# Sparse attention and a mixture of experts on one core: a token list cleared only behind each expert's tokens, weights loaded later, wider value rows

## The chip, the cores and the metric

The kernel runs on one core of a Trainium2 chip. The metric is the time of one execution on the device in microseconds, here the median of three runs. Matrix products run on TensorE (PE in the profile), reductions and elementwise work on VectorE (DVE), activations and casts on ScalarE (ACT), copies and indirect DMAs on GpSimd (POOL); SyncE (SP) issues nearly all direct DMAs. Data lie in the chip's memory (DRAM here), in SBUF (128 partitions) and in PSUM, where TensorE puts its results.

## The reference

```python
def _attn_ref(q, k, v, n_global, n_local):          # q, k, v: (4, 8, 768, 64); 8 globals, window 96
    scores = np.matmul(q, k.transpose(0, 1, 3, 2)) / np.sqrt(D)
    is_global = pos[None, :] < n_global
    is_local = (rel >= 0) & (rel < n_local)         # rel = query position - key position
    dist = np.where(is_global & ~is_local, float(n_local), np.abs(rel))
    scores = scores - slopes[:, None, None] * dist  # slopes = 2 ** -(h + 1), one per head
    scores = np.where(is_global | is_local, scores, -1e9)
    a = softmax(scores)                             # with 1e-9 added to the sum
    return np.matmul(a, v)

def _moe_ref(x, modality_id, w_gate, modality_bias, w1, w2):   # x: (3072, 512), 8 experts
    logits = x @ w_gate + modality_bias[modality_id]
    e_idx = np.argmax(logits, axis=1)
    gate_w = softmax(logits)[e_idx]                 # of the chosen expert
    for e in range(8):                              # w1: (8, 512, 1024), w2: (8, 1024, 512)
        h = np.maximum(x[e_idx == e] @ w1[e], 0.0)
        out[e_idx == e] = gate_w * (h @ w2[e])

def reference(...):                                 # heads of a token side by side: x
    return _moe_ref(_attn_ref(q, k, v, ...).transpose(0, 2, 1, 3).reshape(3072, 512), ...)
```

Everything is float32. Every query sees at most 96 earlier keys and 8 global ones; every token goes to one expert.

## The kernel before, in words

**Attention.** The 3,072 queries (4 batches of 768) are cut into 24 blocks of 128. `step(n)` writes the instructions of one block, with the scores of block n beside the value products of blocks n − 1 and n − 2. For each block SyncE loads queries (`qt`), keys (`kt`) and the value rows twice, once as they are (`va`) and once shifted by 32 positions (`vb`). A value row holds 8 heads of 64 numbers and a one each (`D1` = 65), so 520 floats or 2,080 bytes; `loadv` loads 128 such rows per tile, and `copyv` copies 64 of them on GpSimd into the tile of the block before. TensorE computes scores (L207), transposes probabilities (L274) and multiplies them with the values (L321). The result of a block, `xr`, is written to DRAM as 128 rows of `x_rows` (L352).

**Gate and token lists.** Behind each block come gate logits and the expert choice; behind each batch the positions of its tokens within their experts are worked out (`base` holds the running counts). Each token's number and gate are written by an indirect DMA on GpSimd (`route_c`, L455: 128 rows of 64 bytes from `tki`) into the DRAM list `ids_sorted`, in which every expert has its own stretch of rows. A unit of the second stage is 512 consecutive rows of this list. The last unit of an expert may read past the expert's tokens; it must find zeros there. For that the list is filled with zeros early: `consts_c` writes it from a tile of zeros, `zrow`, in eight DMAs of 196 KB on SyncE, placed at the steps 3 to 10 (`at(n, f)` puts f into step n, `last_work[n]` at the step's end).

**Experts.** A unit reads its list rows (`ld_x`, L594), gathers its rows of x on GpSimd (`gather_x`, L603), loads its expert's weights (`ld_w`: four raw tiles of 512 KB of the first layer, L623, and four of the second, L625), splits x and weights into a high and a low part of a shorter format, and does three products for each (L675 to L677, L714 to L716). Between the layers ScalarE applies the ReLU (L678, `hhe`) and VectorE forms its low part (L679, `hle`); at the end ScalarE scales by the gate (L731, `obe`; two buffers) and GpSimd scatters the rows to the output by an indirect DMA (L732). Two units, `e0` and `e1`, are formed from the first two batches and run first, while the last batch's tokens are still being routed; their tiles are `xge`, `rawe0a`, `rawe0b`, `rawe1a`, `rawe1b`. The next full unit is `s0` (`xgs`, `uis`).

**What sets the order.** TensorE, VectorE, ScalarE and GpSimd issue in the order in which the code is written in the parts around the change. SyncE's queue is put in order by a scheduler from the order in which the DMAs are written and from when their buffers come free. The raw weight tiles come from two pools in turn: `wraw` with 6 buffers, open during the attention, and `wrawb` with 2 buffers, which can be opened only when the attention's pool `a1` is closed. `ld_w` of the first unit's second layer, parts 0 and 1, stands at step `LAST` + 3 (`LAST` = 18), parts 2 and 3 at the end of step `LAST` + 5.

## Time and profile before

| | before |
|---|---|
| runs, us | 460.62, 463.5, 464.26; median 463.5 |
| profiled execution, us | 460.24, span of its instructions 458.4 |
| busy, share of the span | TensorE 92%, VectorE 55%, ScalarE 45%, GpSimd 28% |
| mean granted clock of TensorE | 0.983 |
| moved by DMA | 82.98 MB, of these 69.20 by SyncE's queue, 12.85 by GpSimd's |

All times of the trace below are those of the one profiled execution, counted from its first instruction. The attention's value products end about 165 us after it, and the experts' products fill the rest. A busy TensorE isn't TensorE at its peak, and a share of busy time over the span is a mean over stages with different limits. A wait "issue" is time in which an engine waited for nothing that the profile shows. The DMA share is the mean busy share of the core's 16 DMA engines. A time from issue to landing includes what a transfer waits behind others.

### The profile page before, as it was taken

The numbers are of one execution on the slowest core, as the hardware profiler recorded it, in microseconds if no ns is written. First come the engines' busy times: TensorE is split into PE (matmuls) and PEld (weight loads), VectorE is DVE, ScalarE is ACT, GpSimd is POOL, SyncE is SP. The second block draws the span as 40 slices with busy tenths as digits, with TensorE's granted clock in tenths as the row PEclk, the third lists the DMA queues.
The fourth block names the chain that finished last, engine by engine and source line by source line (L and its number), as shares of the span: only waits on it lengthen the run. The fifth ranks groups of instructions, "written<-read, shape, count | busy, mean of one in ns | idle before, by whom it ended". The sixth has DMA issues, their size and how long they took to land.

```text
span 458.4 us, 13462 instructions
## 1 busy us (share of the span) xinstructions
PE 420.8 (92%) x5391; PEld 337.9 (74%) x5391; DVE 252.4 (55%) x929; ACT 206.4 (45%) x459; POOL 129.5 (28%) x201
## 2 busy tenths in 40 slices
PE   7777989988868799999999999998999999999994
PEld 6565767766656567888888888886888886689983
DVE  5756978769949844887635073508535052331500
ACT  6546676655645332651534153418534152333410
POOL 8231225334355705454301132210100130021001
PEclk9899999999999789999999999999999999999999
DMA  8899987877774710641945162816724253821001
GB/s 275 274 351 338 299 242 242 271 228 229 241 287 143 246 55 4 232 162 52 371 139 200 69 231 75 268 63 220 270 92 162 92 186 118 297 95 46 1 24 51
DMA packets 41322, 82.98 MB, mean 181 GB/s; under 512 B 8571, under 2 KB 10003, under 8 KB 41252
## 3 DMA queue, kind: packets, MB, share of 16 engines
q1 hardware_dynamic: 36580, 69.20, 45.7%
q0 software_dynamic: 4672, 12.85, 7.9%
q8 instruction: 44, 0.72, 0.7%
q14 instruction: 26, 0.21, 0.1%
HBM read 67.64 MB, written 14.45 MB: 179 GB/s over the span
## 4 chain that ended last, share of the span: by engine, by line
PE 44%; issue 17%; POOL 3%; DMA 1%; DVE 0%; ACT 0%; POOLq 0%; DVEq 0%
PE phs L677 3%; PE phs L676 3%; PE phs L675 3%; PE phe L675 3%; PE poe L714 3%; PE pos L716 3%; PE poe L716 3%; PE pos L714 3%; PE poe L715 3%; PE pos L715 3%; PE phe L676 3%; PE phe L677 3%; POOL out L732 2%; DMA xge<-x_rows,uie 1%; PE mts L658 1%
## 5 line engine op out<-in xcount | busy, mean ns | idle before, releaser
L244 ACT ACTIVATE pr<-sc,nmx 128x128 f32<-128x128 f32 x192 | 61.0, 393 | 2.9 <-DVE nmx L228 2.9
L679 DVE SCALAR_TENSOR_TENSOR hls<-phs,hhs 128x512 fp32r<-128x512 f32 (+1 forms) x32 | 21.0, 658 | 71.2 <-ACT hhs L678 71.2
L675 PE MATMUL phs<-xhs,ahs 128*128 128x512 f32 (+1 forms) x128 | 48.4, 378 | 0.0
L677 PE MATMUL phs<-xhs,als 128*128 128x512 f32 (+1 forms) x128 | 48.1, 376 | 0.0
L714 PE MATMUL pos<-bhs,hhs 128*128 128x512 f32 x120 | 48.1, 400 | 0.0
L676 PE MATMUL phs<-xls,ahs 128*128 128x512 f32 (+1 forms) x128 | 48.1, 375 | 0.0
L716 PE MATMUL pos<-bhs,hls 128*128 128x512 f32 x120 | 46.9, 391 | 0.0
L715 PE MATMUL pos<-bls,hhs 128*128 128x512 f32 x120 | 46.8, 390 | 0.0
L228 DVE CUSTOM_DVE_ANT_0 sc<-s,tbl 128x136 f32<-128x136 f32 x192 | 44.2, 294 | 2.6 <-PE s L207 1.9
L732 POOL DMA_INDIRECT out<-obs,ois x15 | 14.9, 994 | 99.7 <-ACT obs L731 99.7
L207 PE MATMUL s<-kt,qt 64*32 64x136 f32 x1536 | 33.6, 283 | 7.9 <-issue 6.3
L678 ACT ACTIVATE hhs<-phs 128x512 fp32r<-128x512 f32 (+1 forms) x32 | 18.3, 572 | 48.7 <-PE phs L677 48.7
L455 POOL DMA_INDIRECT ids_sorted<-tki,pi x24 | 24.3, 1011 | 49.5 <-PE s L368 20.2
L321 PE MATMUL x<-vb,pT 128*32 128x65 f32 x768 | 31.0, 230 | 4.1 <-issue 2.2
L321 PE MATMUL x<-va,pT 128*32 128x65 f32 x768 | 30.8, 230 | 4.1 <-issue 4.0
L321 PEld LDWEIGHTS x<-vb,pT 128*32 128x32 f32 x768 | 27.5, 115 | 8.1 <-issue 5.4
L207 PEld LDWEIGHTS s<-kt,qt 64*32 64x32 f32 x1536 | 23.9, 106 | 12.3 <-issue 9.0
L281 ACT COPY pT<-pt 128x512 f32<-128x512 f32 x24 | 14.1, 586 | 40.5 <-PE pt L274 40.4
L274 PE MATMUL pt<-ident,pr 128*128 128x128 f32 x192 | 27.6, 285 | 4.4 <-ACT pr L244 2.8
L731 ACT ACTIVATE obs<-pos,uis 128x512 f32<-128x512 f32 x15 | 10.4, 692 | 43.5 <-PE pos L716 33.5
L321 PEld LDWEIGHTS x<-va,pT 128*32 128x32 f32 x768 | 27.2, 115 | 3.7 <-issue 3.5
L116 POOL COPY va<-va 64x520 f32<-64x520 f32 x24 | 14.7, 613 | 50.8 <-issue 42.5
(333 smaller groups left out, 972.4 us busy)
## 6 DMA issues: line engine op xcount, KB each, us to landing
va<-in_vr SPq DMA_DIRECT2D x25, 260.0 KB, 4.9
vb<-in_vs SPq DMA_DIRECT2D x25, 260.0 KB, 4.5
qt<-in_qs SPq DMA_DIRECT2D x24, 256.0 KB, 4.2
x_rows<-xr SPq DMA_DIRECT2D x24, 256.0 KB, 4.8
kt<-in_ks SPq DMA_DIRECT2D x20, 272.0 KB, 4.0
rawe0a<-in_moe_w SPq DMA_DIRECT2D x4, 512.0 KB, 5.6
rawe0b<-in_moe_w SPq DMA_DIRECT2D x4, 512.0 KB, 6.7
rawe1a<-in_moe_w SPq DMA_DIRECT2D x4, 512.0 KB, 5.3
```

The lines of the kernel that those rows point to most:

```text
L207: nc.tensor.matmul(ps[h][32 * j : 32 * j + 32, hp % 2 * W : hp % 2 * W + W], qt[hs, hp, 32 * j : 32 * j + 32], keys, start=True, stop=True,)
L228: V.tensor_tensor_reduce(out=sc, in0=pss[n, hp // 2][h][:, hp % 2 * W : (hp % 2 + 1) * W], in1=(tbl0 if n % NB == 0 else tbl)[:, hh, :], o ...
L244: last[0] = nc.scalar.activation(four(prs[n][:, hh, :], 32), four(scs[n][:, hx(hh), :])[:, :, 0:32], AF.Exp, bias=blk[n][:, hx(hh) : hx(hh ...
L274: nc.tensor.transpose(tp[:, j * P : (j + 1) * P], prs[n][:, hh, :], ident)
L321: nc.tensor.matmul(px[h][js, hp * D1 : (hp + 1) * D1], pT_of(n, hh)[:, js], vj[j][:, hh, :], start=False, stop=(hp == NP - 1), skip_group_ ...
L455: ins = nc.gpsimd.indirect_dma_start(out=ids, out_offset=bass.IndirectOffsetOnAxis(ap=pi[:, j : j + 1], axis=0), in_=tki[:, b * NB + j, :] ...
L675: nc.tensor.matmul(o, hi[:, fs], s.xh[:, c, 0:n], start=(c == 0), stop=False)
L676: nc.tensor.matmul(o, hi[:, fs], s.xl[:, c, 0:n], start=False, stop=False)
L677: nc.tensor.matmul(o, lo[:, fs], s.xh[:, c, 0:n], start=False, stop=(c == 3))
L714: nc.tensor.matmul(s.po[t], s.hh[:, fc, tt], hi[:, wv], start=(fc == 0), stop=False)
L715: nc.tensor.matmul(s.po[t], s.hh[:, fc, tt], lo[:, wv], start=False, stop=False)
L716: nc.tensor.matmul(s.po[t], s.hl[:, fc, tt], hi[:, wv], start=False, stop=(fc == 7))
```

## The change

Three edits.

1. *The list.* Each expert's stretch gets `ST` = 3,072 + 128 rows. The eight writes of zeros are gone; one write of 32 KB clears rows 0 to 511. A new function, `clear_ends`, is called once all counts are final: for each expert it computes the row behind its last token plus the partition number and writes 128 rows of zeros there, by one indirect DMA on GpSimd each, eight in all. Scatters of tokens and clears never touch the same rows, and are declared independent of each other.
2. *The first unit's second-layer weights.* Parts 0 and 1 are loaded at the end of the last step instead of step `LAST` + 3; parts 2 and 3 once `wrawb` is open.
3. *Value rows.* `vr` and `vs` are laid out with 528 floats (2,112 bytes) per row instead of 520, the last 8 unused; tiles `va` and `vb` have that width, and `copyv` copies 520.

```diff
-    ids = nc.dram_tensor("ids_sorted", (E * NT + U, IDW), I32, kind="Internal").ap()
+    ids = nc.dram_tensor("ids_sorted", (E * ST + U, IDW), I32, kind="Internal").ap()
...
-    va = [a1.tile([P, H, D1], F32, name=f"va{i}") for i in range(NV)]
+    va = [a1.tile([P, DV], F32, name=f"va{i}") for i in range(NV)]
...
-    nid = (E * NT + U) * IDW // P
-    zrow = a2.tile([P, nid // 8], I32, name="zrow")
-
-    def consts_c(j):
-
-        if not j:
-            nc.gpsimd.memset(zrow, 0)
-        idv = ids.rearrange("(p r) w -> p (r w)", p=P)
-        nc.sync.dma_start(idv[:, j * nid // 8 : (j + 1) * nid // 8], zrow)
+    zid = const.tile([P, U // P * IDW], I32, name="zid")
+
+    def consts_c():
+
+        nc.gpsimd.memset(zid, 0)
+        nc.sync.dma_start(ids[0:U].rearrange("(p r) w -> p (r w)", p=P), zid)
+
+    def clear_ends(pool, cnt):
+
+        end = pool.tile([P, E], F32, name="end")
+        V.tensor_tensor(end, cnt, ebase, ALU.add)
+        endi = pool.tile([P, E], I32, name="endi")
+        V.tensor_scalar(endi, end, pidx, None, ALU.add)
+        made = []
+        for e in range(E):
+            ins = nc.gpsimd.indirect_dma_start(
+                out=ids,
+                out_offset=bass.IndirectOffsetOnAxis(ap=endi[:, e : e + 1], axis=0),
+                in_=zid[:, 0:IDW],
+                in_offset=None,
+            )
+            for prev in made:
+                tc.declare_no_dep(ins.ins, prev.ins, reason="each expert has rows of its own")
+            made.append(ins)
+        return made
...
-    for j in range(8):
-        at(3 + j, consts_c, j)
+    at(3, consts_c)
...
-    at(LAST + 3, lambda: ld_w(eslots[0], "b", (0, 1)))
-    last_work[LAST + 5] = [(lambda: [gather_x(eslots[0], mark[0], (2, 3)), ld_w(eslots[0], "b", (2, 3))], ())]
+    last_work[NBLK] = [(lambda: ld_w(eslots[0], "b", (0, 1)), ())]
+    last_work[LAST + 5] = [(lambda: gather_x(eslots[0], mark[0], (2, 3)), ())]
...
     wrawb = sM.enter_context(tc.tile_pool(name="wrawb", bufs=RB, side="right", reuse_waits="tile"))
+    ld_w(eslots[0], "b", (2, 3))
...
+        for ins in clear_ends(plan, base[:, B - 1, NB, :]):
+            for prev in scat:
+                tc.declare_no_dep(ins.ins, prev.ins, reason="rows behind the last token of an expert")
+        yield
         r = yield from rest_plan(base[:, B - 1, NB, :], first_used)
...
-    laid["vr"] = rows.reshape(B, S, H * D1)
+    laid["vr"] = _np.zeros((B, S, DV), v.dtype)
+    laid["vr"][..., 0 : H * D1] = rows.reshape(B, S, H * D1)
```

The order of instructions on TensorE and ScalarE stays the same. Three places where it moves follow; a row is a source line, an operation and its operands, and line numbers of the change are two higher.

SyncE around the first unit's first-layer weights, before:

```order
L623 DMA rawe0a_3166<-in_moe_w 128x1024
L623 ISA
L623 DMA rawe0a_3168<-in_moe_w 128x1024
L352 DMA x_rows<-xr_3057 128x512
L99 DMA qt_3227<-in_qs 128x512
L625 ISA
L625 DMA rawe0b_3472<-in_moe_w 128x2x512
L625 ISA
L625 DMA rawe0b_3474<-in_moe_w 128x2x512
L592 TENSOR_LOAD uoie
```

and with the change:

```order
L625 DMA rawe0a_3159<-in_moe_w 128x1024
L625 ISA
L625 DMA rawe0a_3161<-in_moe_w 128x1024
L354 DMA x_rows<-xr_3050 128x512
L101 DMA qt_3220<-in_qs 128x512
L594 TENSOR_LOAD uoie
```

The two second-layer loads have left the place behind the last query block; the loads of the first-layer weights ahead of them stay.

SyncE from the reading of the unit's list rows (`uie`) on, before:

```order
L594 DMA uie_3543<-ids_sorted 128x4x2
L594 ISA
L594 DMA uie_3554<-ids_sorted 128x4x2
L625 ISA
L625 DMA rawe0b_3884<-in_moe_w 128x2x512
L352 DMA x_rows<-xr_3728 128x512
L625 ISA
L625 DMA rawe0b_3886<-in_moe_w 128x2x512
L352 DMA x_rows<-xr_3878 128x512
L623 ISA
L623 DMA rawe1a_4224<-in_moe_w 128x1024
```

and with the change:

```order
L596 DMA uie_3543<-ids_sorted 128x4x2
L627 ISA
L627 DMA rawe0b_3959<-in_moe_w 128x2x512
L627 ISA
L627 DMA rawe0b_3961<-in_moe_w 128x2x512
L354 DMA x_rows<-xr_3717 128x512
L354 DMA x_rows<-xr_3867 128x512
L354 DMA x_rows<-xr_3955 128x512
L627 ISA
L627 DMA rawe0b_4046<-in_moe_w 128x2x512
L627 ISA
L627 DMA rawe0b_4048<-in_moe_w 128x2x512
```

Parts 0 and 1 stand where part 2 stood, parts 2 and 3 behind the last three writes of `x_rows`; the second unit's first-layer loads (`rawe1a`) come only behind them.

GpSimd behind the gathers of the second unit, before:

```order
L455 DMA ids_sorted<-tki,pi_4153 25088x16 x6
L603 DMA xge_4240<-x_rows,uie_3554 128x512 x4
L732 DMA out<-obe_4469,oie_4172 3072x512
L455 DMA ids_sorted<-tki,pi_4343 25088x16 x6
L732 DMA out<-obe_4607,oie_4172 3072x512
L732 DMA out<-obe_4637,oie_4172 3072x512
```

and with the change:

```order
L457 DMA ids_sorted<-tki,pi_4146 26112x16 x6
L605 DMA xge_4233<-x_rows,uie_3543 128x512 x4
L1078 DMA ids_sorted<-zid,endi 26112x16 x8
L734 DMA out<-obe_4465,oie_4165 3072x512
L457 DMA ids_sorted<-tki,pi_4336 26112x16 x6
L734 DMA out<-obe_4612,oie_4165 3072x512
L734 DMA out<-obe_4642,oie_4165 3072x512
```

The eight clears (L1078) stand ahead of the first output and of the last batch's six scatters.

## Rows read from the trace of the kernel before

**Rows 1.** Windows: stretch, length, busy us per engine, granted clock, DMA share, GB/s

```profile
27.00:46.00 19.00, 15.27 (x485) 11.53 (x468) 12.16 (x75) 10.79 (x36) 4.45 (x9) 1.00 1.02 345
46.00:92.00 46.00, 42.34 (x1393) 33.32 (x1392) 37.84 (x228) 31.03 (x98) 16.71 (x35) 1.00 0.84 263
...
117.00:145.00 28.00, 20.33 (x629) 15.67 (x632) 20.69 (x113) 15.60 (x49) 12.62 (x15) 1.00 0.75 253
145.00:168.00 23.00, 18.77 (x385) 14.62 (x367) 15.97 (x52) 8.24 (x21) 11.64 (x19) 0.78 0.48 157
168.00:458.00 290.00, 282.14 (x1340) 230.30 (x1338) 128.16 (x245) 110.31 (x158) 59.44 (x58) 1.00 0.41 140
```

**Rows 2.** Waits of PE, 27 to 46 us: total, times, longest

```profile
PE x L321 <- issue: 1.6, 2, 1.1
PE pt L274 <- issue: 1.1, 1, 1.1
PE s L207 <- issue: 0.7, 1, 0.7
```

**Rows 3.** Timeline of SP's DMA issues: start, us, line, transfer, count

```profile
27.97 2.66 SPq L1068 DMA_DIRECT2D ids_sorted<-zrow  x4
...
121.55 1.29 SPq L625 DMA_DIRECT2D rawe0b<-in_moe_w  x2
...
150.37 0.37 SPq L625 DMA_DIRECT2D rawe0b<-in_moe_w  x1
...
153.91 1.89 SPq L623 DMA_DIRECT2D rawe1a<-in_moe_w  x2
```

**Rows 4.** DMA queues: kind, packets, MB, share of 16 engines

```profile
q8 instruction: 44, 0.72, 0.7%
```

**Rows 5.** Timeline of PE: start, us, work, [idle before <- releaser]

```profile
127.61 0.22 PE L321 MATMUL x<-va,pT 128*32 128x65 f32 x1 [2.01 <-issue]
...
133.94 0.55 PE L274 MATMUL pt<-ident,pr 128*128 128x128 f32 x3 [2.80 <-ACT pr L244]
```

**Rows 6.** Timeline of ACT ahead of the second of these

```profile
131.67 1.28 ACT L244 ACTIVATE pr<-sc,nmx 128x128 f32<-128x128 f32 x4
```

**Rows 7.** Waits of PE, 145 to 168 us

```profile
PE mte L658 <- DMA xge<-x_rows,uie: 1.6, 2, 1.1
```

**Rows 8.** DMA issues by transfer: count, KB each, median us from issue to landing

```profile
va<-in_vr SPq DMA_DIRECT2D x25, 260.0 KB, 4.9
vb<-in_vs SPq DMA_DIRECT2D x25, 260.0 KB, 4.5
...
kt<-in_ks SPq DMA_DIRECT2D x20, 272.0 KB, 4.0
...
ids_sorted<-tki,pi POOLq DMA_INDIRECT x24, 2.3
...
out<-obe,oie POOLq DMA_INDIRECT x8, 2.8
```

**Rows 9.** Timeline of POOL: first output, last of six scatters

```profile
198.91 1.03 POOL L732 DMA_INDIRECT out<-obe,oie  x1 [9.68 <-ACT obe L731]
...
207.14 0.97 POOL L455 DMA_INDIRECT ids_sorted<-tki,pi  x1 [0.30 <-issue]
```

**Rows 10.** Timeline of ACT: first cast, fourth output scaling, first ReLU of e1

```profile
183.27 1.05 ACT L645 CAST bhe<-rawe0b 128x1024 fp32r<-128x1024 f32 x1
...
214.83 0.69 ACT L731 ACTIVATE obe<-poe,uie 128x512 f32<-128x512 f32 x1 [4.75 <-PE poe L716]
217.50 0.60 ACT L678 ACTIVATE hhe<-phe 128x512 fp32r<-128x512 f32 x1 [1.98 <-PE phe L677]
```

**Rows 11.** Timeline of DVE: behind the final counts, and e1's first low part

```profile
195.82 1.23 DVE L646 TENSOR_TENSOR ale<-rawe1a,ahe 128x1024 fp32r<-128x1024 f32 x1
...
218.13 0.69 DVE L679 SCALAR_TENSOR_TENSOR hle<-phe,hhe 128x512 fp32r<-128x512 f32 x1 [2.60 <-ACT hhe L678]
```

**Rows 12.** Timeline of PE: fifth block of e1's first layer, first transpose of s0

```profile
225.46 0.39 PE L675 MATMUL phe<-xhe,ahe 128*128 128x512 f32 x1
...
239.07 0.60 PE L658 MATMUL mts<-ident,xgs 128*128 128x128 f32 x4
```

## The prediction

> **What bounds the kernel now.** I read the windows first [rows 1]. From 168 us to the end TensorE is busy 282.14 of 290 us with the two layers of the experts at a granted clock of 1.00: work to be done, and the change leaves that engine's order as it is. What can be won lies ahead of it, in the attention stages, where TensorE is busy 15.27 of 19, 42.34 of 46, 20.33 of 28 and 18.77 of 23 us. Whatever makes the attention end earlier moves the whole rest forward, since the expert stage has next to no idle time that could swallow it.

> Next, the waits of TensorE by stretch. From 27 to 46 us its idle time is put down to "issue", 1.6 + 1.1 + 0.7 = 3.4 us [rows 2]: no engine and no transfer that the profile links to an instruction released it. In this stretch the DMA engines are at a share of 1.02, 345 GB/s, and the issues of SyncE show why: eight writes of zeros of 196 KB, the first four at 27.97 [rows 3], go out among the loads of the blocks.

> What is such an "issue" wait? The queues hold a candidate: 44 packets, 0.72 MB, so 16 KB each, of kind instruction [rows 4]. The engines' programs come through the same DMA engines as the data. If TensorE's next piece of program stands behind data, TensorE stands still and nothing in the dependences shows it. This is a reading, not a fact. For it: such waits lie where the DMA share is high. The stretch from 168 on has a share of 0.41 and an idle time of 7.86 us in 290.

> The stretch from 117 to 145 has the two longest ones: TensorE resumes at 127.61 after 2.01 us of "issue", and at 133.94 after 2.80 us [rows 5]. The second is put down to ScalarE's exponentials, but the four of them began at 131.67 and took 1.28 us together [rows 6], so they were over at 132.95, 1.0 us before TensorE went on. Here too something else came last. Ahead of both, at 121.55, SyncE issues two loads of the first unit's second-layer weights (`rawe0b`), 512 KB each [rows 3], behind 2 MB of its first-layer weights. Last, from 145 to 168, TensorE waits 1.6 us for the gather of the unit's rows (`xge`) [rows 7], while the fourth such load (150.37) and two first-layer loads of the second unit (153.91) are on their way [rows 3].

> **The sum, part by part**, against the profiled run's 460.24 us (span 458.4), which is 3.3 below the median of 463.5; I take the difference over to the median.

> *Zeros.* 1.57 MB leave the stretch from 27 to 46. At its 345 GB/s that is 4.6 us of transfers. TensorE's 15.27 us of work, at the next stretch's busy share (42.34/46 = 0.92, DMA share 0.84), would take 16.6 instead of 19 us [rows 1]: −2.4. At most all the issue waits go, −3.4; at least one of 0.7 [rows 2]. I take −2.4, the next stretch being the nearest picture of the same work without zeros. The 32 KB that remain cost nothing that shows.

> *Second-layer weights 0 and 1.* Two loads, 1 MB, leave the place at 121.55 and come behind the reads of the lists, where one such load stood before. The 2.01 us wait I leave standing: the 2 MB of first-layer weights are still ahead of it. The 2.80 us wait stands behind the removed megabyte (3.0 us at 345 GB/s); I take −2.7, with 0 and −4.8 (both waits) as ends. In the new place a megabyte could make a wait of its own, up to 2.0 as at 127.61. I take 0: the DMA share from 145 to 168 is 0.48, the lowest of the attention stretches [rows 1]. What hides their later landing: ScalarE casts the first of them at 183.27 [rows 10], 40 us later.

> *Weights 2 and 3.* They move behind the attention's last value product, and on SyncE's queue the four first-layer loads of the second unit now stand behind them. Both pairs have cover: they are read from 183.27 on [rows 10], and the second unit's first-layer weights only once the first unit is computed. If that cover went, the price would be a landing, some 5 us. The gathers `xge` lose 1.5 MB of competitors: their wait of 1.6 can go whole (−1.6) or stay (0). I take −1.6. [...]

> *Value rows.* 50 loads grow by 1.5%, 0.2 MB in all, 0.6 us of transfers at 345 GB/s, spread over 24 blocks. No row shows this width. The nearest ones: `va` lands in 4.9 us and `vb` in 4.5, `kt` with rows of 2,176 bytes and 272 KB in 4.0 [rows 8]. So longer rows aren't dearer as such, and between +0.6 and a gain (rival B) I take +0.3. [...]

> *The clears.* Two VectorE steps more, and eight indirect DMAs on GpSimd between the second unit's gathers and the first output. There GpSimd is idle (9.68 us ahead of the output at 198.91), and a scatter of the same kind takes 0.97 us of it, 1.27 with the gap behind it [rows 9]: 8 × 1.27 = 10.2 us. The counts are final with the vector step before 195.82 [rows 11]; with that step's 1.23 and the two new ones the clears start at 197.6 and end at 207.8. What is queued behind them: output 0 (to 209.1), six scatters (7.6, to 216.7), output 1, which lands 2.8 us later [rows 8], at 219.5. It frees the buffer for ScalarE's fourth output scaling, at 214.83 before (0.7); behind that on ScalarE stands the ReLU of 217.50 (0.6) [rows 10], then VectorE's step of 218.13 (0.69) [rows 11]. That chain now ends at 221.5. TensorE wants the PSUM bank for 225.46 [rows 12]: 3.9 us to spare, cost 0. The list read and the gathers behind these outputs slip by up to 5 us; their first reader stands at 239.07 [rows 12], 24 us behind the scaling. Bounds: 0, and rival C.

> Sum: −2.4 −2.7 −1.6 −0.5 +0.3 = −6.9, so 453.3 for a run like the profiled one and **456.5** against the median. The ends that I hold likely together give 452 to 460.

> **Rivals.**
> A: the issue waits aren't made by this traffic. Against it speaks that the stretch with the zeros has the highest share; for it, that the stretch from 117 to 145, at 0.75, idles more than that from 46 to 92, at 0.84: 7.67 of 28 us against 3.66 of 46 [rows 1]. Also, a wait that goes may only return at the next piece of program. What is left is the gather's 1.6: **462**. [...]

> B: the wider rows also land faster. If `va` and `vb` came down to the 4.0 of `kt` [rows 8], each block's loads would be through 0.9 and 0.5 us sooner, and the 2.01 us wait that I left standing [rows 5] and half of the 3.66 us of idle time from 46 to 92 [rows 1] might go as well. I estimate another 4 us: **452.5**. For it speaks only that the narrower row is the slower one; against it, that `kt` is also fetched at other moments.

> C, the slower side: the clears hold GpSimd longer than the scatters did. With c for each clear and scatter the chain above ends at 203.7 + 14c; from c = 1.55 on it passes 225.46. Were each to hold the engine for the 2.3 us of its landing [rows 8], it would end at 235.9 and TensorE stand for 10.5 us. With the fetch terms at their low ends (0.7 and 0) and the gather's 1.6: **471**. Against it speaks that six scatters in a row were issued at 1.27 [rows 9]; for it, that fourteen in a row don't occur before.

> **Numbers.** Forecast 0.55, A 0.25, B 0.13, C 0.07. The range from 450 to 463.5 leaves out C, the lowest part of B and the upper edge of A. Some 1% of the time (4.6 us) is what a measurement of this kernel can tell from no change. The forecast passes it in five sixths of its cases (0.46), B always, A hardly (0.03): faster 0.62. C gives slower nearly always: 0.07. The rest, 0.31, is within 1%.

> **What would show it.** Right: TensorE's issue waits between 27 and 46 us fall to about 1; the wait before the transposes at 133.94 is gone while the 2.01 us one stays; no `xge` wait; the fourth output scaling held for some 5 us until the second output has landed, and no idle time of TensorE before its step at 225.46. Wrong: waits of the same length at other places in the attention (A); `va` and `vb` landing near 4.0 (B); TensorE released by ScalarE or VectorE in the second unit's first layer (C). What would make it wrong most simply is that a fetch, put off no longer by zeros, meets the next block's loads instead.

## The result, and the profile after

The changed kernel took 457.81 us (median of 15 runs, 454.85 to 460.69), the kernel before 464.77 us (15 runs, 460.62 to 467.14): ratio 0.9858, 95% interval 0.9827 to 0.9888, so 6.6 us less by the ratio. The forecast was −6.9. On another chip the very same program was 1.7% slower than the kernel before; that is the last experiment, and the more important half of what follows.

The profiled execution of the change has a span of 454.7 us, 3.7 less than that of before. One execution of each says less than the medians: the profiled run of before (460.24) lies 4.5 below its median.

Windows of the change (columns as in [rows 1]); the last two rows are a second cut, around the second unit's first layer:

```profile
27.00:46.00 19.00, 15.94 (x495) 12.29 (x495) 12.32 (x75) 11.11 (x36) 4.32 (x8) 0.92 0.85 282
46.00:92.00 46.00, 41.95 (x1343) 32.44 (x1343) 36.50 (x222) 29.96 (x96) 15.96 (x33) 1.00 0.81 246
...
117.00:145.00 28.00, 24.61 (x806) 19.71 (x805) 22.83 (x124) 17.64 (x57) 14.80 (x20) 0.97 0.71 231
145.00:168.00 23.00, 19.34 (x370) 14.14 (x356) 16.55 (x53) 9.53 (x24) 11.33 (x18) 0.93 0.67 223
168.00:454.00 286.00, 278.60 (x1317) 227.67 (x1315) 126.29 (x243) 108.61 (x155) 69.98 (x66) 1.00 0.42 140
...
166.00:215.00 49.00, 49.00 (x242) 39.81 (x241) 35.69 (x138) 17.58 (x27) 26.73 (x26) 1.00 0.29 104
215.00:237.00 22.00, 22.00 (x101) 18.23 (x100) 11.56 (x17) 10.71 (x16) 9.25 (x8) 1.00 0.79 283
```

The gain stands where the weights were: from 117 to 145 us TensorE gets 806 matmuls done instead of 629, and from 145 to 168 the granted clock is 0.93 instead of 0.78. Since the two kernels have drifted apart by then, a window no longer holds the same work in both; counted from the start, the change is 135 matmuls behind at 117 us and 24 ahead at 168. From 27 to 46, where the zeros were, the DMA share fell from 1.02 to 0.85 and the traffic from 345 to 282 GB/s, yet TensorE's busy time rose only from 15.27 to 15.94 us, and from 46 to 92 it did 50 matmuls fewer than before.

TensorE's waits in the change, of the stretches 27 to 46 (three rows), 117 to 145, 145 to 168 and 168 to the end:

```profile
PE pt L276 <- issue: 1.6, 1, 1.6
PE x L323 <- issue: 0.8, 1, 0.8
PE s L209 <- issue: 0.7, 1, 0.7
...
PE x L323 <- issue: 1.6, 1, 1.6
...
PE x L323 <- POOL vb L119: 1.9, 1, 1.9
PE mte L660 <- DVE xle L664: 1.0, 1, 1.0
...
PE pog L718 <- DVE hlg L708: 1.7, 2, 0.9
```

Against [rows 2]: 3.1 us of issue waits from 27 to 46 where there were 3.4. Against [rows 5]: the wait of 2.80 us is gone, the one of 2.01 is there with 1.6. Against [rows 7]: no wait for `xge`, but 1.0 us for VectorE's split of the same rows. The 1.9 us put down to GpSimd's copy of value rows (`vb`) isn't new; the trace of before has it from 145 to 168 us too:

```profile
PE x L321 <- POOL vb L117: 1.9, 1, 1.9
```

So the megabyte that now stands behind the list reads made no wait of its own. Behind 168 us TensorE waits for nothing that the clears could have made.

How transfers land, and the data queue (columns as in [rows 8]):

```profile
q1 hardware_dynamic: 35572, 67.83, 46.0%
...
va<-in_vr SPq DMA_DIRECT2D x25, 264.0 KB, 3.0
vb<-in_vs SPq DMA_DIRECT2D x25, 264.0 KB, 2.8
```

The medians of `va` and `vb` look like a large gain from the wide rows (4.9 and 4.5 in [rows 8]). They are medians of those few loads that something waited for, three of each here, seven and eight before. The queue shows no gain: 46.0% of 16 engines' 454.7 us for 67.83 MB, 49.3 us of an engine per MB; before it was 45.7% of 458.4 us for 69.20 MB, 48.4.

The clears in the timeline of the change: first clear, second output, fourth output scaling and first ReLU of the second unit, the fifth block of its first layer, and SyncE's first loads for the next unit:

```profile
194.17 0.99 POOL L1078 DMA_INDIRECT ids_sorted<-zid,endi  x1 [8.49 <-DVE lib L504]
...
214.09 1.00 POOL L734 DMA_INDIRECT out<-obe,oie  x1 [0.30 <-issue]
...
217.07 0.69 ACT L733 ACTIVATE obe<-poe,uie 128x512 f32<-128x512 f32 x1 [8.45 <-DMA out<-obe,oie]
217.66 0.59 ACT L680 ACTIVATE hhe<-phe 128x512 fp32r<-128x512 f32 x1
...
221.90 0.39 PE L677 MATMUL phe<-xhe,ahe 128*128 128x512 f32 x1
...
215.90 2.58 SPq L625 DMA_DIRECT2D raws0a<-in_moe_w  x4
```

The chain over GpSimd went as forecast: the fourth scaling waits 8.45 us for the second output, the ReLU follows at once, and TensorE goes on without a gap 4.2 us later.

### The profile page after: what moved, and what is told of

Read it like the earlier page. It is cut to its first block, busy times and chain, and to the rows that moved or that the text cites. A ratio compares the mean times of both kernels' runs of the same rounds, so it can differ in the third digit from the quotient of the medians.

```text
span 454.7 us, 13466 instructions
## 1 busy us (share of the span) xinstructions
PE 420.7 (93%) x5391; PEld 336.9 (74%) x5391; DVE 251.3 (55%) x931; ACT 206.3 (45%) x459; POOL 139.8 (31%) x209
## 3 DMA queue, kind: packets, MB, share of 16 engines
q1 hardware_dynamic: 35572, 67.83, 46.0%
## 4 chain that ended last, share of the span: by engine, by line
issue 33%; PE 25%; POOL 6%; DVE 1%; DMA 1%; POOLq 0%; ACT 0%; SPq 0%
POOL out L734 3%; PE phe L677 3%; PE poe L716 3%; PE poe L718 3%; PE phe L679 3%; PE poe L717 3%; PE phe L678 3%; POOL xgs L605 2%; PE phs L678 1%; PE phs L677 1%; PE phs L679 1%; DMA uis<-ids_sorted 1%; PE x L323 1%; PE mte L660 1%; PE mts L660 0%
## 5 line engine op out<-in xcount | busy, mean ns | idle before, releaser
L677 PE MATMUL phs<-xhs,ahs 128*128 128x512 f32 (+1 forms) x128 | 48.4, 378 | 0.0
L209 PE MATMUL s<-kt,qt 64*32 64x136 f32 x1536 | 34.9, 290 | 7.4 <-issue 5.8
L733 ACT ACTIVATE obs<-pos,uis 128x512 f32<-128x512 f32 x15 | 10.4, 692 | 43.5 <-PE pos L718 33.2
```

Source lines behind the costliest of these rows:

```text
L209: nc.tensor.matmul(ps[h][32 * j : 32 * j + 32, hp % 2 * W : hp % 2 * W + W], qt[hs, hp, 32 * j : 32 * j + 32], keys, start=True, stop=True,)
L677: nc.tensor.matmul(o, hi[:, fs], s.xh[:, c, 0:n], start=(c == 0), stop=False)
```

## The experiments

Four groups of runs, each on one chip, with the kernel before on the same chip. The last column is read from each profile's timeline: the time from the first product of the first unit's second layer (`poe`) to the first transpose of the next unit (`mts`); before, 190.80 to 239.07 = 48.27.

| run | what | ratio to before, 95% | `poe` to `mts`, us |
|---|---|---|---|
| the change | | 0.9858 (0.9827 to 0.9888) | 48.26 |
| e1, chip 2 | clears alone | 1.0164 (1.0125 to 1.0203) | 56.36 |
| e2, chip 2 | weights alone | 0.9915 (0.9883 to 0.9947) | 48.25 |
| e3, chip 2 | rows alone | 1.0010 (0.9975 to 1.0044) | 48.25 |
| e4, chip 2 | all but the clears | 0.9926 (0.9896 to 0.9955) | 48.27 |
| e5, chip 15 | all but the weights | 1.0015 (0.9980 to 1.0049) | 48.28 |
| e6, chip 15 | clears alone, late | 0.9992 (0.9955 to 1.0030) | 48.28 |
| e7, chip 15 | the change, clears late | 0.9881 (0.9829 to 0.9932) | 48.26 |
| e8, chip 15 | the change, GpSimd delayed | 0.9876 (0.9825 to 0.9926) | 48.26 |
| e9, chip 5 | clears alone again | 1.0173 (1.0125 to 1.0221) | 56.91 |
| e10, chip 5 | the change and 1 MB of copies | 1.0158 (1.0122 to 1.0194) | 56.89 |
| e11, chip 5 | the change, first-layer loads spaced | 1.0082 (1.0045 to 1.0120) | 57.31 |
| e12, chip 0 | the change again | 1.0172 (1.0127 to 1.0217) | 57.90 |

**One edit at a time (e1 to e4).** Each is the kernel before with the hunks of one edit, e4 with those of two:

```diff
 e2:
-    at(LAST + 3, lambda: ld_w(eslots[0], "b", (0, 1)))
+    last_work[NBLK] = [(lambda: ld_w(eslots[0], "b", (0, 1)), ())]
...
+    ld_w(eslots[0], "b", (2, 3))
 e3:
+DV = H * D1 + 8
 e1 (and left out in e4):
-        at(3 + j, consts_c, j)
+        for ins in clear_ends(plan, base[:, B - 1, NB, :]):
```

> The kernel before with the first edit alone: eight writes of zeros (1.57 MB) out of 27 to 36 us, eight clears on GpSimd at 198 us. Theory 1 (the forecast: TensorE's program stood behind the zeros): -2.4 us, ratio 0.995, and fewer issue waits of TensorE from 27 to 46 us. Theory 2 (the waits come back at the next pieces of program, as in the one profile of the change, where block 7 of the attention begins at 46.96 instead of 46.16 us): 0 +- 1 us, ratio 1.000, the sum of issue waits over the attention as before. Theory 3 (the edit carries the whole gain): -6.5 us, ratio 0.986.

> The kernel before with the second edit alone: second-layer weights of the first unit loaded at the end of the last step and behind the attention. Theory 1 (the forecast: -2.7 for the program that stood behind them, -1.6 for the gather, -0.5 for the clock): -4.8 us, ratio 0.990; the wait of 2.8 us before the transposes of block 20 is gone. Theory 2 (only the gather and the clock behind the attention): -2 to -3 us, ratio 0.995. Theory 3 (rows or zeros carry the gain): 0, ratio 1.000.

> The kernel before with the third edit alone: value rows of 2,112 bytes. Theory 1 (the forecast): +0.3 us, ratio 1.000 to 1.001, the queue of SyncE takes 1.5% longer for these rows. Theory 2 (rival B: wider rows land faster and the program fetches behind them too): -3 to -4 us, ratio 0.992.

> The change without its first edit: the eight writes of zeros are back, the weights are late and the value rows wide. If the edits add up and theory 1 of each holds: ratio to before 0.990 (-4.5 us). If the zeros cost nothing that lasts: 0.986, as the whole change. If the zeros carry the gain: 1.000.

Rows: no change in time, theory 1. Weights: −0.85%, 4.0 us, near theory 1's 4.8. Clears alone: none of the three theories; 1.6% slower. The table's last column says where: 8.1 us between `poe` and `mts`, a stretch whose length is otherwise the same to 0.03 us. e4 came out as the first of its three ratios (0.990, if the edits add up). It is e2 with wide rows, and both have the zeros: that they agree says once more that the rows do nothing, and nothing of the zeros.

**Does the order on GpSimd make that loss? (e5 to e8)** e5 leaves the weights at their old places, so it is e1 with wide rows. e6 and e7 hold the clears behind the second output, e8 lengthens the chain:

```diff
 e6, e7:
+        while len(scaled) < 2:
+            yield
         for ins in clear_ends(plan, base[:, B - 1, NB, :]):
+            behind(ins, scaled[1])
 e8, in clear_ends:
+        nc.gpsimd.tensor_copy(idle, bm(end, 256))
```

> The change without its second edit: clears and wide rows, the first unit's second-layer weights at their old places. The clears alone had cost 1.6%, and the change with everything but the clears had gained 0.7%, the whole change 1.4%. Theory 1 (the clears only pay when the weights are late: with the old places the second unit's first layer stands still between 230 and 240 us): ratio to before 1.014 to 1.018, and a stretch from the first unit's second layer to the next unit's transposes of some 56 us instead of 48. Theory 2 (the loss of the clears alone was an accident of that program's placement in time, and the edits add up): ratio 0.992 to 1.000.

> The kernel before with the first edit alone, the eight clears on GpSimd held behind the second output scaling, so that they stand behind the six scatters and the second output instead of ahead of them; wide rows and late weights left out. Theory 1 (the clears ahead of the second output hold ScalarE's fourth scaling and with it TensorE in the second unit's first layer): the 8 us that the clears alone lost come back, ratio 0.995 to 1.000, no idle time of TensorE between 225 and 245 us. Theory 2 (the loss has nothing to do with GpSimd's order): ratio 1.016 as with the clears ahead.

> The whole change, the eight clears behind the second output. Theory 1 (in the whole change the chain over GpSimd has slack left, and the clears cost nothing where they are): same as the change, ratio to before 0.983 to 0.989; the gathers of the next unit come some 5 us later and still ahead of their reader. Theory 2 (the clears cost something in the change as well): below 0.983.

> The whole change with one copy of 128 x 2048 numbers more on GpSimd ahead of the clears, some 2.4 us, so that clears, scatters and the second output come about as late as in the kernel with the clears alone. Theory 1 (a chain with 3.9 us of slack as forecast): no loss, ratio to before 0.983 to 0.990. Theory 2 (the point from which it decides lies lower, between the change and the clears alone, and behind it the loss is 8 us at once): ratio 1.000 to 1.006, TensorE standing in the second unit's first layer.

e5: theory 2, no loss; edits that lost 1.6% on chip 2 lose nothing on chip 15. e6 can therefore not tell its theories apart: there was nothing to bring back. e7 and e8 are as the change: with the clears moved out of the chain or with the copy ahead of it (1.90 us in the profile, by which the first clear comes 1.7 us later behind the first `poe`) nothing changes. Of the 3.9 us of slack that the forecast gave the chain, at least these 1.7 are there.

These four also measure the weights a second time, on one chip and without the long stretch: e8 against e5 (0.9876 to 1.0015) and e7 against e6 (0.9881 to 0.9992) differ by the place of the weights, and otherwise only by edits that cost nothing here. That is 1.4 and 1.1%, some 6 and 5 us, more than e2's 4.0, though with ratios known to some 0.5% the two measurements don't exclude each other.

**Repeat, and two tests of traffic (e9 to e11).** e9 is e1, word for word. e10 adds traffic at the old place of the weights, e11 spreads the 2 MB that are left there:

```diff
 e10:
+            nc.sync.dma_start(
+                spd[c],
+                w2[ds(eslots[0].e, 1), 2 * c * P : 2 * (c + 1) * P, :].rearrange("o (a p) d -> p (o a) d", p=P),
+            )
 e11:
-    last_work[LAST] = [(lambda: ld_w(eslots[0], "a", (0, 1)), ())]
+    last_work[LAST + 1] = [(lambda: ld_w(eslots[0], "a", (1,), last[0]), ())]
```

> The kernel with the clears alone once more, word for word the same. It had lost 1.6%, of this 8.1 us in one place of the experts' stage where TensorE, ScalarE and SyncE went forward in steps of 0.7 us for 8 us; the same edit with wide rows beside it lost nothing. Theory 1 (the loss belongs to this program, whatever run it is): ratio 1.013 to 1.020, the same place, 56 us from the first unit's second layer to the next unit's first transpose. Theory 2 (it belonged to that loading of the program): ratio 0.995 to 1.003, and 48.3 us there.

> The whole change, with two copies of 512 KB each from DRAM to DRAM more on SyncE's queue, at the place from which the second-layer weights were taken; nothing reads what they write, so that nothing but the traffic is added. Theory 1 (1 MB of traffic at this place makes TensorE wait, through its program's fetch and the loads behind it): 2 to 4 us of the gain are lost, ratio to before 0.992 to 0.996, and an issue wait of 2.5 us or more is back between 120 and 140 us. Theory 2 (the gain came from the gathers and the clock behind the attention alone): as the change, 0.986 to 0.988.

> The whole change, the first unit's four first-layer loads (2 MB, issued within 4 us before) one to a block of the attention. Theory 1 (traffic in a lump makes the waits): the wait of some 1.6 to 2.0 us that the change left in block 20 goes, -1.5 to -2 us against the change, ratio to before 0.982 to 0.985. Theory 2 (the wait comes back at the next pieces of program, as with the zeros): as the change, 0.986 to 0.988. Theory 3 (the last load comes too late for GpSimd's cast, and the gathers behind it): slower than the change.

e9 lost the same 1.7% in the same place. e10 and e11 carry the clears, and both have the long stretch too, which neither expectation had foreseen, so their totals against before say little about traffic. What can be read is TensorE's waits between 117 and 145 us. The first fence is of e10, the second of e11 (its last two rows, behind the dots, are of 145 to 170 us), the third, for comparison, of the change on chip 0 (e12):

```profile
PE x L324 <- issue: 4.1, 6, 2.3
```

```profile
PE x L323 <- issue: 2.4, 6, 0.5
...
PE x L306 <- DVE xr L347: 2.3, 1, 2.3
PE x L323 <- issue: 1.1, 1, 1.1
```

```profile
PE x L323 <- issue: 3.5, 4, 2.4
```

With the megabyte put back the longest wait is 2.3 us, without it 2.4: no wait of 2.5 us or more came back, against theory 1. Both stand where the trace of before waits 2.01 us, behind the first-layer loads; what the megabyte did at the place of the 2.80 us is told below, under "What an issue wait is". Spread, the longest wait there falls to 0.5, as theory 1 has it, but the two rows behind it, of 145 to 170 us, show what is late next: 2.3 us for VectorE's `xr` and an issue wait of 1.1. On the same chip e11 took 470.06 us and e10 473.36.

**The chip or the program? (e12)** By then the profiles fell in two kinds. In one, nearly every scatter on GpSimd during the attention is followed by a short stop of TensorE; in the other none is.

> The change itself once more, unaltered. In seven kernels of two of the three earlier groups of runs (chips 2 and 5) TensorE stands still for some 0.5 us at the end of nearly every indirect DMA of GpSimd in the attention, and the four of them that have the clears lose 8 to 9 us in the second unit's first layer; in the other group (chip 15) and in the change's own profile neither shows. Theory 1 (it belongs to the chip on which a program runs, not to the program): if the short stops show on this chip, the change has 56 to 57 us there instead of 48.3 and is at 1.004 to 1.012 of the kernel before; if they don't, it is at 0.984 to 0.990 with 48.3 us. Theory 2 (it belongs to the programs): no short stops and no long one, 0.984 to 0.990 on any chip.

The change itself, unaltered, at 1.0172: theory 1. Its timeline; first two pairs of a scatter and the stop behind it, then the second unit's first layer:

```profile
77.84 0.98 POOL L457 DMA_INDIRECT ids_sorted<-tki,pi  x1 [1.52 <-PE s L370]
79.15 0.22 PE L323 MATMUL x<-va,pT 128*32 128x65 f32 x1 [0.43 <-issue]
83.74 0.98 POOL L457 DMA_INDIRECT ids_sorted<-tki,pi  x1 [2.71 <-PE s L370]
85.06 0.24 PE L323 MATMUL x<-vb,pT 128*32 128x65 f32 x1 [0.46 <-issue]
...
199.40 1.00 POOL L1078 DMA_INDIRECT ids_sorted<-zid,endi  x1 [10.60 <-DVE lib L504]
...
219.90 1.00 POOL L734 DMA_INDIRECT out<-obe,oie  x1 [0.30 <-issue]
...
222.79 0.69 ACT L733 ACTIVATE obe<-poe,uie 128x512 f32<-128x512 f32 x1 [7.85 <-DMA out<-obe,oie]
231.38 0.60 ACT L680 ACTIVATE hhe<-phe 128x512 fp32r<-128x512 f32 x1 [7.89 <-remote]
...
222.78 0.48 PE L677 MATMUL phe<-xhe,ahe 128*128 128x512 f32 x1 [0.59 <-issue]
224.22 0.47 PE L678 MATMUL phe<-xle,ahe 128*128 128x512 f32 x1 [0.95 <-issue]
225.66 0.41 PE L679 MATMUL phe<-xhe,ale 128*128 128x512 f32 x1 [0.97 <-issue]
...
228.87 0.95 POOL L605 DMA_INDIRECT xgs<-x_rows,uis  x1 [0.30 <-issue]
...
224.18 5.72 SPq L625 DMA_DIRECT2D raws0a<-in_moe_w  x4
```

The stops end 1.31 and 1.32 us after the scatter began. Of the 12 indirect DMAs between 70 and 142 us, 9 have an idle time of TensorE of over 0.25 us that ends 1.1 to 1.6 us after their start; in e2 it is 10, in the change's own profile none, in that of before one (the 2.80 us of [rows 5]). The short stops belong to the attention: in the experts' stage GpSimd starts 26 indirect DMAs between 175.93 and 219.90, and TensorE has no idle time of over 0.06 us until 222.19. From 199.40 to 228.87 GpSimd issues one after another. From 222 us on TensorE goes forward by one or two matmuls in 1.4 us, ScalarE does not begin a ReLU whose input was complete, and SyncE takes 5.72 us for the four issues that took 2.58. GpSimd itself keeps its rhythm of 0.95 to 1.01 us. Windows of the same program on this chip:

```profile
168.00:218.00 50.00, 50.00 (x246) 40.36 (x245) 35.39 (x138) 17.38 (x27) 24.77 (x24) 1.00 0.34 114
218.00:240.00 22.00, 17.59 (x57) 12.44 (x56) 8.06 (x11) 7.13 (x10) 8.14 (x9) 0.77 0.66 227
240.00:460.00 220.00, 218.32 (x1036) 178.65 (x1035) 84.07 (x98) 84.58 (x120) 33.98 (x33) 1.00 0.42 138
```

In 22 us 57 matmuls instead of the 101 that the change did in its window of 215 to 237, partly at the lower clock (0.77): in windows of a few us the granted clock is 0.99 from 222 to 226, 0.50 from 226 to 236 and 0.98 from 236 to 240, so for some 10 us behind the first stops it stands at 0.50. 57.90 − 48.26 = 9.6 us are lost here; the median is 8.2 us over that of before (472.66 against 464.43), so all else still gives about 1.4.

What sets the long stop off: of the eight kernels profiled with short stops (e1 to e4, e9 to e12) the five that have the clears have it, and the three that don't (e2, e3, e4) have not; of the five programs with the clears profiled without short stops (the change, e5 to e8) none has it. In these thirteen it takes both. By what path GpSimd's indirect DMAs hold three other engines is not shown, nor whether it is the chip or how a program was loaded on it; no run distinguishes these. Clears behind the second output (e6, e7) ran only on chip 15, so whether moving them avoids the long stop is not known either.

## Why the prediction was right, and which steps failed

**The size** −6.9 against −6.6 is right, within the forecast's own range of 452 to 460, but in part by luck: where no short stops show, the weights gave some 5 to 6 us by e5 to e8, more than their −4.8, and the zeros nothing of their −2.4. (The forecast's 456.5 should read 456.6 by its own sum.)

**What an issue wait is.** The prediction called it a reading that TensorE waits for its program there; the traces bear it out. Number the records of TensorE's queue (weight loads, matmuls and the some 90 waits and branches between them) in order of start: of its 20 idle times of over 0.35 us between 9 and 140 us in the trace of before, 15 come at the same place, record 193 or 194 of every 256; in the change 13 of 16. 16 KB a packet [rows 4] and 256 records from place to place make an estimated 64 bytes a record. The trace also has the times of the 16 KB packets: each of these 15 waits ends 1.25 to 1.60 us after the end of a packet, one packet to each such place. The wait of 2.80 us is one of them: its packet came from 131.56 to 132.53, and TensorE went on at 133.94. The short stops of e12 are something else: none of its nine stands at such a place.

The same packets show what holds a fetch up. Count from TensorE's passing one such place to the start of the packet for the next. At the place of the 2.80 us this is 3.3 to 4.2 us in the seven profiles with a megabyte at the old place (before, e1, e3, e5, e6, e9 with the weights, e10 with the copies) and 1.0 to 1.8 in the six without it (the change, e2, e4, e7, e8, e12). So the megabyte held the fetch up by some 2.5 us, as the forecast had it, and in e10 it did so again, though little of it became a wait there (0.4 us). At the place before, behind the 2 MB of first-layer loads, it is 3.4 to 4.6 us in thirteen profiles and 1.5 in e11, which spreads them.

**Zeros, −2.4: not there.** e6, the first edit without the long stretch, is at 0.9992 (0.9955 to 1.0030), and −2.4 would be 0.9948; e5 (1.0015) against e3 (1.0010) says the same. The step that failed is taking the next stretch as the picture of this one without zeros. The traffic fell and the issue waits stayed (3.1 for 3.4 us). With the zeros gone SyncE issues the blocks' loads sooner: the `qt` of 35.30 us goes out at 31.11. The four fetches that start between 28 and 43 us began 3.60, 2.14, 2.30 and 2.53 us behind the place before on the mean of the four profiles with zeros, and 3.62, 2.35, 2.66 and 1.78 on that of the ten without: 10.6 and 10.4 in sum. So a fetch is held up as long as before, by all appearance by the loads that moved up; the prediction's last sentence named this as what would make it wrong most simply.

**Weights, −2.7 −1.6 −0.5 = −4.8: right in mechanism, and about right in size.** e2 measures −4.0 (2.5 to 5.5 by its interval of 0.9883 to 0.9947, against 466.47 for before on that chip), e5 to e8 some 5 to 6. From the program place that TensorE passes at 120.81 in the trace of before to the one at 137.56, around both long waits, the three profiles without short stops and with early weights (before, e5, e6) take 17.8 us on their mean, the three with late ones (the change, e7, e8) 14.2: −3.6 for the forecast's −2.7. With short stops (e1, e3, e9 against e2, e4, e12) it is 16.6 and 15.7, −0.9. From there to the first unit's second layer the six with early weights take 52.4 us and the six with late ones 50.3, −2.1 as forecast for the gather and the clock together. These are single profiles, which differ among themselves by 1 to 4 us. The `xge` wait is gone in every kernel with late weights (and in e6). No run shows the −0.5 for the clock, which was the author's estimate: from 145 to 168 us the granted clock is 0.78 to 1.00 in the profiles with early weights and 0.85 to 1.00 in those with late ones.

**Rows, +0.3: right.** e3, +0.1% (−0.25 to +0.44). Rival B falls by that. Its sign, landing medians near 4.0, tells nothing: the change has 3.0 and 2.8 for `va` and `vb`, e7 with the same rows 4.4 and 4.7, and e6 with the narrow ones 4.8 and 3.0.

**Clears, 0: right where it was measured, wrong elsewhere.** The price c was 1.28 us between most clears and 1.34 on their mean, the chain closed with slack, and e8 used up 1.7 us of it at no cost in time. Rival C named the place and the outcome, TensorE standing in the second unit's first layer and a kernel slower by 1.6%, but not the mechanism: c is, but for two of the eight clears, the same 0.95 to 1.0 + 0.30 in e12, and what TensorE loses there comes from no wait that the chain contains.

## What to carry to other kernels

The long series of small indirect DMAs on GpSimd wasn't free here, although GpSimd was idle before it (10.60 us ahead of the first clear in e12): on three of the four chips with recorded numbers it held up TensorE, ScalarE and SyncE and cost 8 to 10 us, with no wait in the chain that could announce it. A gain of 1.5% measured on one chip should be repeated on a second before it is kept; here the safe part is the late weights alone (0.9915 on a chip where the whole change loses). And traffic was taken here from two stretches whose waits sit at fixed places of the program: where the zeros had been, other loads moved up and the issue waits stayed (3.1 for 3.4 us); where the weights had been, none held the program up, and the wait of 2.80 us went. So what will move up into the place should be looked at first.
